# When weight halves are loaded and rounded in the first batch of a spectral mixing and SwiGLU kernel

## The chip, the cores and the metric

The kernel runs on one core of one Trainium2 chip. The metric is the device time of one execution in microseconds (us). Engine names are those of the profile: PE is TensorE (PEld its weight loads), DVE is VectorE, ACT is ScalarE, POOL is GpSimd, SP is SyncE; ACTq and SPq are instructions by which ACT and SP issue DMA transfers.

## What is computed

The reference has two parts, one after the other. `x` has shape (8, 3008, 256), the weights have 256 x 1536 and 1536 x 256 elements.

```python
X = np.fft.rfft(x, axis=1)
y = np.fft.irfft(X * (filt_r + 1j * filt_i)[None], n=3008, axis=1)
t = y.reshape(24064, 256)
g = t @ w_gate
out = (g / (1 + np.exp(-g)) * (t @ w_val)) @ w_out
```

The reference's weights are double precision numbers. The kernel reads them as pairs of 32-bit words and rounds them to single precision itself.

## The kernel before

**The transform.** The length 3008 is 47 x 64. A `Spectral` object stands for one of the 8 batches. Stage 1 (`stage1`; `stage1_first` and `turn` for batch 0) and stage 2 (`stage2a`: product with a table, then with the filter; `stage2b`: product with a second table) write their result to DRAM as `d2`: `stage2b(u)` copies its sum to a buffer `g` on ACT and stores it, 12 stores for a batch, each of eight rows of `d2_rows`, which has 96. `load_t4` reads `d2_rows` back and `stage3` makes the inverse transform over 47 from it, in four steps for each group of tokens: step s has token half i = s // 2 and channel half cb = s % 2. A step with cb = 0 is copied by ACT to the first four parts of the tile `y`; a step with cb = 1 is combined with those by DVE and ACT into the last four parts.

**The feed forward layer.** The products with `w_val`, `w_gate` and `w_out` are made by a fast bilinear scheme: sums and differences of parts of `y` (the tile `y_t`, by `combine_sequence`) are multiplied with sums and differences of weights (`wt_t`, and in batch 0 also `lent`). One pass over a group of tokens `k` and a third `g` of the hidden units is a step of 12 in a batch, and its order is written out by hand in the list `SCHEDULE` of 150 tokens: `P`, `Q`, `A`, `B`, `E` are products (L731: `wk`, `wa`, `we`), `f`, `c`, `m`, `D`, `x`, `s`, `y`, `e`, `l`, `g`, `u`, `h`, `v`, `S` are the work of ACT, DVE and POOL on them, `W` and `o` the projection with `w_out` (L810 and the sums behind it), and `t` runs a piece of the next batch's transform. Batch 0 takes its first nine steps as (0,0), (1,0), (2,0), (0,1), (1,1), (2,1), (0,2), (1,2), (2,2) in (k, g).

**The weights in batch 0.** The weights come in 36 halves of 256 KB: for each of three groups eight halves of hidden weights and four of `w_out`. `load_weights(i)` fetches half i, `round_half(i)` rounds it in pieces, separated by `yield`. Halves 0 to 11 (`N_EARLY`) are loaded early by SyncE; the others are loaded by a DMA instruction in ACT's queue. From half 12 on three of five use places in the tail of `wo_t` (`spot_of`) and the others, with all of the last four halves (`N_LENT` is 32), two buffers `raw`. The last four halves are `w_out`.

`Preparation` lays all of this out in ticks: each half has a start `b`, its pieces run at fixed ticks after `b`, and its load stands some ticks before. The class writes it so:

```python
gap = 4 if i != 2 * len(BLOCKS) and i != len(weights) - 2 else 8
b = base[-1] + gap if i else 0
...
last = base[same[-k]] + 8 if same[k - 1:] else 0
put(max(last, b - 10), lambda i=i: load_weights(i), by)
```

`same[-k]` is the half that used the buffer before. Eight ticks are run by stage 1 of batch 0, 24 by its stage 2 loop, the rest up to tick 46 by `preparation.finish(0)`, and after that 20 ticks in each step, spread evenly over the tokens; tick 100 is not run before step 3, so that step 3 begins at tick 100, step 4 at 120, step 5 at 140 and step 6 at 160.

**The start of batch 0.** SyncE issues, in this order: the input `x`, tables and the first eight halves, `wi_t`, halves 8 to 11, and then the stores of `stage2b` for u up to 9 (the others stand in ACT's queue). Then it loads `d2` back in two parts: rows 0 to 79 and rows 80 to 95 (`load_t4` with `part`). While these come, TensorE runs products that only keep it busy (`warm`, `idle`).

Engines work through their queues in the order in which the code gives them (`pin`). Of SyncE's later work the transfers that matter here are `load_x` (L482), the stores and reloads of `y` (L922, L926), of sums (L929, L932), of rounded weights (L371) and of partial outputs (L695, L794).

Of the kernel before, what the change touches and what calls it, by code (L numbers as in the profile page):

```python
# [56 lines left out]
NK = 4 * NS  # L57
# [6 lines left out]
NT = 3  # L64
NG = 3
# [6 lines left out]
N_TWO = NS // NV  # L72
# [27 lines left out]
BLOCKS = (0, 1, 3, 2)  # L100
# [44 lines left out]
def kernel(  # L145
# [10 lines left out]
    nc = tc.nc  # L156
    wf_host, wi_host, de_host = dft_tables()
    wf_dram = nc.inline_tensor(wf_host, name="wf_tbl")
    wi_dram = nc.inline_tensor(wi_host, name="wi_tbl")
# [17 lines left out]
    wi_t = cpool.tile([NK, NR], FP32)  # L177
# [44 lines left out]
    pin = tc.keep_in_program_order  # L222
# [37 lines left out]
    weights = list(weight_halves())  # L260
    raws = {}
# [12 lines left out]
    N_EARLY = 12  # L274

    def load_weights(i):
        if i in raws or i >= len(weights):
            return
        if i < N_EARLY:
            raws[i] = early_raw(i)  # L280
        elif spot_of(i) is not None:
            raws[i] = bits(4 * 7 * 128 + 512 * spot_of(i))
        else:
            raws[i] = rpool.tile([128, 2, 128, 2], U32, name=f"raw_{i}", tag="raw", bufs=2)
        queue = nc.sync if i < N_EARLY else nc.scalar
        pin(queue.dma_start(out=raws[i], in_=weights[i][0]))

    def round_half(i):


        raw, (use, *at) = raws[i], weights[i][1]
        low, high = raw[:, :, :, 0], raw[:, :, :, 1]
        pw = rpool.tile([128, 2, 128], U32, name=f"pw_{i}", tag="pw", bufs=3)
        if i % 3 == 2 and i < N_LENT:
            w = wo_t.rearrange("p j i f -> p (j i f)")[:, NJ * 7 * 128 - 256:]
            w = w.rearrange("p (b f) -> p b f", b=2)
        else:
            w = rpool.tile([128, 2, 128], FP32, name=f"w_{i}", tag="w", bufs=2)
        man = w.bitcast(U32)
        v = nc.vector  # L300
        flat = "p b f -> p (b f)"
        flat2 = "p b f two -> p (b f) two"
        pin(v.tensor_scalar(out=man, in0=high, scalar1=0xFFFFF, scalar2=None,
                            op0=ALU.bitwise_and))
        yield
        pin(v.tensor_scalar(out=pw, in0=high, scalar1=20, scalar2=0x7FF,
                            op0=ALU.logical_shift_right, op1=ALU.bitwise_and))
        pin(nc.scalar.activation(out=w, in_=man, func=AF.Copy, scale=2.0 ** -20, bias=1.0))
        yield
        pf = pw.bitcast(FP32)  # L310
        pin(nc.scalar.activation(out=pf, in_=pw, func=AF.Relu, bias=off_t))
        pin(nc.scalar.activation(out=pf, in_=pf, func=AF.Relu, bias=top_t, scale=-1.0))
        yield
        pin(nc.scalar.activation(out=pw, in_=pf, func=AF.Copy, scale=-(2.0 ** 23),
                                 bias=255 * 2.0 ** 23))
        yield
        pin(v.scalar_tensor_tensor(out=pw.rearrange(flat), in0=raw.rearrange(flat2)[:, :, 1],
                                   scalar=0x80000000, in1=pw.rearrange(flat),
                                   op0=ALU.bitwise_and, op1=ALU.bitwise_or))
        yield  # L320
        pin(v.scalar_tensor_tensor(out=w.rearrange(flat), in0=raw.rearrange(flat2)[:, :, 0],
                                   scalar=2.0 ** -52, in1=w.rearrange(flat),
                                   op0=ALU.mult, op1=ALU.add))
        yield
        e = nc.gpsimd
        if use == "proj":
            j, l = at
            dst = wo_t[:, j]
            pin(e.tensor_tensor(out=dst[:, ts(l, 2), :], in0=w, in1=pf, op=ALU.mult))
            yield  # L330
            if l:
                b11, b12, b21, b22, t1, t2, t4 = [dst[:, i] for i in range(7)]
                pin(sub(e, t1, b12, b11))
                pin(sub(e, t2, b22, t1))
                pin(sub(e, b12, b22, b12))
                pin(sub(e, t4, b21, t2))
            return
        g, i, z = at
        wt = weights_of(0, 0, g)
        x, y, u = w[:, 0], wt[:, SLOT[f"Q{i}"], z], wt[:, SLOT[f"P{i}"], z]  # L340
        pin(e.tensor_tensor(out=y, in0=w[:, 1], in1=pf[:, 1], op=ALU.mult))
        pin(e.tensor_tensor(out=x if KS[i] else u, in0=x, in1=pf[:, 0], op=ALU.mult))
        yield
        if KS[i] == -1:
            pin(sub(e, u, x, y))
        elif KS[i]:
            pin(add(e, u, x, y))
            if KS[i] == 2:
                pin(add(e, u, u, y))
# [27 lines left out]
    class Preparation:  # L377
# [3 lines left out]
        def __init__(self):  # L381
            self.at, self.held = 0, []

            self.ticks, self.need = {}, {}
            base, ready = [], {}

            def put(t, f, by, pool=False):
                self.ticks.setdefault(t, ([], []))[pool].append(f)
                self.need[by] = max(self.need.get(by, 0), t)

            for i, (_, (use, *at)) in enumerate(weights):
                hid, g = use == "hid", at[0] if use == "hid" else at[0] // JB
                by = ((0, 3, 6) if hid else (1, 4, 7))[g]
                gap = 4 if i != 2 * len(BLOCKS) and i != len(weights) - 2 else 8
                b = base[-1] + gap if i else 0
                base.append(b)
                if hid and g == NG - 1:
                    ready.setdefault(NT, b)
                if i >= N_EARLY:
                    same = [n for n in range(N_EARLY, i) if spot_of(n) == spot_of(i)]  # L400
                    k = 2 if spot_of(i) is None else 1
                    last = base[same[-k]] + 8 if same[k - 1:] else 0
                    put(max(last, b - 10), lambda i=i: load_weights(i), by)
                half = []

                def go(half=half, i=i):
                    if not half:
                        half.append(round_half(i))
                    next(half[0], None)

                for n, t in enumerate((0, 1, 2, 3, 6, 7, 9, 10)):
                    put(b + t, go, by, n > 5)
                if hid and at[1:] == [BLOCKS[-1], 1]:
                    for n, pair in enumerate(PAIRS_USED):
                        c = combine_weights(g, *pair)
                        for t in range(3):
                            put(b + 11 + n + t, lambda c=c: next(c, None), by, t == 2)
            self.barriers = sorted((t, step) for step, t in ready.items())
            self.end = max(self.ticks)
# [50 lines left out]
    class Spectral:  # L470
# [59 lines left out]
        def load_t4(self, k, i, part=None):  # L530
            if part is not None:

                t = f0[0:NK, ts(i, NH), :]
                r = (slice(0, NK - 16), slice(NK - 16, NK))[part]
                self.load(out=t[r], in_=self.d2_rows[r, ts(i, NH), :])
            else:
                t = t4pool.tile([NK, NH, C], FP32, name=f"t4_{self.b}_{k}_{i}", tag="t4")
                self.load(out=t, in_=self.d2_rows[:, ts(2 * k + i, NH), :])
            self.t4[k, i] = t
# [78 lines left out]
        def stage2b(self, u):  # L618

            pt, tb = self.p.pop(u), self.tb.pop(u)  # L620
            ps = self.bank(f"pc_{self.b}_{u}")
            for i in range(NV):
                pin(nc.tensor.matmul(out=ps[:, i, :], lhsT=tb[:, i, 1, :],  # L623
                                     rhs=pt[:, i, :], start=True, stop=True))
            g = self.place("g", u)
            yield
            pin(nc.scalar.copy(out=g, in_=ps))
            queue = nc.scalar if self.b or u > N_TWO - 3 else nc.sync
            pin(queue.dma_start(out=self.twos(self.d2, u), in_=g))

        def stage3(self, k, step):
# [207 lines left out]
    with tc.tile_pool(name="start", bufs=1) as spool0:  # L839
# [12 lines left out]
        n = 0  # L852
# [23 lines left out]
                ("w", 7), ("t", 5)]  # L876
        for what, i in load:
            {"x": spec.load_x, "w": load_weights, "t": spec.load_tables}[what](i)
        pin(nc.sync.dma_start(out=wi_t, in_=wi_dram.ap()))
        for u in range(8):  # L880
            if u in (4, 6):
                idle(zero, [bank("idle") for _ in range(2)], 512)
            spec.stage1_first(u)
            if u > 3:
                preparation.tick(0, 2)
        for i in range(8, N_EARLY):
            load_weights(i)
        for u in range(2):
            spec.turn(u)
        lag = 3  # L890
        for u in range(N_TWO + lag):
            if u < N_TWO:
                spec.turn(u + 2)
                step = spec.stage2a(u)
# [5 lines left out]
                spec.real_part(u + 1)  # L900
            if u >= lag:
                run(spec.stage2b(u - lag))
            if u == N_TWO:
                for i in range(2):
                    spec.load_t4(0, i, 0)
        for i in range(2):
# [2 lines left out]
            spec.load_t4(1, i)  # L909
        preparation.finish(0)  # L910
        warm()
        for step in range(4):
            run(spec.stage3(0, step))
        idle(zero, [bank("idle") for _ in range(3)], 512)
        following = Spectral(1)
# [77 lines left out]
    for b in range(B):  # L993
# [33 lines left out]
        for step in range(NCHUNK * NG + (b == B - 1)):  # L1027
# [17 lines left out]
            for place, token in enumerate(SCHEDULE):  # L1045
# [5 lines left out]
                if op[0] == "t":  # L1051
                    n = int(op[1])
# [60 lines left out]
```

## Time and profile before

| | |
|---|---|
| time, median of 3 | 2984.84 us (2982.82 to 2984.92) |
| span of the profiled run | 2983.5 us |
| PE busy | 2932.4 us (98%) |
| DVE, ACT, POOL busy | 1929.5, 1616.7, 1584.0 us |
| bytes read from and written to HBM | 459.73 MB and 95.05 MB |

A line of a timeline has the start, the length, the engine, the line of the code, the operation, what it writes and reads, the shapes, how many such instructions were merged (x), and in brackets how long the engine stood idle before it and what released it. A line of the windows has the stretch, its length, the busy time and number of instructions of PE, PEld, DVE, ACT and POOL, the TensorE clock that was granted (1.00 is full), the share of the 16 DMA engines and GB/s. In the page the span is cut into 40 slices of 75 us; each digit is a share in tenths.

Step 0 of batch 0 begins at about 88 us; steps 1 to 6 begin at 117.1, 151.65, 187.14, 218.29, 264.18 and 301.66 us.

### The profile page before, as it was taken

To read this page: it belongs to the slowest core of one execution; us is meant where nothing else is said; L and a number is where in the kernel's file an instruction comes from. 1 tells how busy PE (TensorE), PEld (TensorE's weight loads), DVE (VectorE), ACT (ScalarE), POOL (GpSimd) and SP (SyncE) were. 2 spreads that over 40 slices of the span, in tenths; PEclk is the share of its full clock that TensorE was granted. 3 is DMA by queue.
4 is the path that set the end of the run, shared out by engine and by line. 5 is a ranking of instruction groups with operands and counts; after the bars stand their busy time and mean duration, and the time that the engine had idled before them with its cause. 6 is when DMAs were issued, how large, how long until landed. Compare 5 with 4: busy or idle time off the path is not lost.

```text
span 2983.5 us, 57655 instructions
## 1 busy us (share of the span) xinstructions
PE 2932.4 (98%) x20292; PEld 2832.4 (95%) x20292; DVE 1929.5 (65%) x4379; ACT 1616.7 (54%) x4207; POOL 1584.0 (53%) x1764
## 2 busy tenths in 40 slices
PE   7898999999999999999999999999999999999999
PEld 5887999999999999999999999999999999999999
DVE  6786775566655766557665577656676566666665
ACT  5775455555555555555555555555545555555554
POOL 3875564454554555455644464545564545555453
PEclk9998999999999999999999999999999999999999
DMA  8575875565645665556555566556665565644442
GB/s 209 184 259 182 270 248 170 176 211 184 209 154 191 206 200 173 180 183 219 180 178 182 186 216 196 168 179 192 199 204 165 178 201 187 207 151 146 142 135 89
DMA packets 217082, 558.60 MB, mean 187 GB/s; under 512 B 29872, under 2 KB 107552, under 8 KB 216512
## 3 DMA queue, kind: packets, MB, share of 16 engines
q1 hardware_dynamic: 165994, 479.82, 50.8%
q10 hardware_dynamic: 41872, 51.20, 5.1%
q0 software_dynamic: 8928, 23.89, 2.3%
q8 instruction: 163, 2.67, 0.4%
q14 instruction: 125, 1.02, 0.1%
HBM read 459.73 MB, written 95.05 MB: 186 GB/s over the span
## 4 chain that ended last, share of the span: by engine, by line
PE 89%; DMA 0%; DVE 0%; SPq 0%; issue 0%; ACT 0%; POOL 0%; ACTq 0%; DVEq 0%
PE wa L731 23%; PE wA L810 16%; PE wk L731 15%; PE we L731 12%; PE wG L810 8%; PE wF L810 4%; PE pd L639 3%; PE pa L551 3%; PE pc L623 2%; PE pb L591 2%; DMA lent<-de_tbl 0%; DMA y<-y 0%; DVE o L225 0%; POOL D L228 0%; SPq L695 0%
## 5 line engine op out<-in xcount | busy, mean ns | idle before, releaser
L731 PE MATMUL wa<-y_t,wt_t 128*128 128x188 f32 x4464 | 882.0, 324 | 10.3 <-ACT m L766 3.3
L731 PEld LDWEIGHTS wa<-y_t,wt_t 128*128 128x128 f32 x4464 | 731.4, 190 | 36.0 <-issue 16.3
L225 POOL TENSOR_TENSOR h<-h 128x376 f32<-128x376 f32 x190 | 183.0, 985 | 797.6 <-DVE h L778 797.6
L810 PE MATMUL wA<-wo_t,h 128*128 128x128 f32 x4608 | 579.2, 276 | 2.4 <-DVE o L225 2.0
L810 PEld LDWEIGHTS wA<-wo_t,h 128*128 128x128 f32 x4608 | 564.0, 192 | 16.7 <-issue 10.7
L731 PE MATMUL wk<-y,wt_t 128*128 128x188 f32 x2976 | 567.2, 323 | 0.0
L228 POOL TENSOR_TENSOR h<-h 128x376 f32<-128x376 f32 x570 | 554.5, 995 | 0.5
L731 PEld LDWEIGHTS wk<-y,wt_t 128*128 128x128 f32 x2976 | 478.6, 190 | 25.7 <-issue 20.2
L228 DVE TENSOR_TENSOR we<-we,m 128x376 f32<-128x376 f32 x576 | 318.5, 556 | 196.2 <-PE we L731 140.3
L731 PE MATMUL we<-y_t,wt_t 128*128 128x188 f32 x2232 | 431.5, 323 | 0.1
L731 PEld LDWEIGHTS we<-y_t,wt_t 128*128 128x128 f32 x2232 | 369.5, 190 | 0.6 <-DVE we L232 0.4
L228 POOL TENSOR_TENSOR D<-f,f 128x376 f32<-128x376 f32 x288 | 280.3, 987 | 105.4 <-ACT f L746 104.7
L232 DVE SCALAR_TENSOR_TENSOR y<-wk,c 128x376 f32<-128x376 f32 x480 | 244.9, 542 | 134.8 <-ACT we L762 84.8
L766 ACT COPY m<-wa 128x376 f32<-128x376 f32 x576 | 272.0, 472 | 87.7 <-PE wa L731 86.6
L773 ACT ACTIVATE g<-wa 128x188 f32<-128x188 f32 x576 | 188.2, 327 | 191.1 <-PE wa L731 181.7
L810 PE MATMUL wG<-wo_t,h 128*128 128x128 f32 x2304 | 289.9, 276 | 0.6 <-DVE o L225 0.6
L773 ACT ACTIVATE u<-we 128x188 f32<-128x188 f32 x576 | 189.2, 328 | 175.5 <-DVE we L228 156.3
L810 PEld LDWEIGHTS wG<-wo_t,h 128*128 128x128 f32 x2304 | 283.1, 193 | 1.0 <-DVE o L225 0.8
L746 ACT ACTIVATE f<-wk 128x376 f32<-128x376 f32 x288 | 139.4, 484 | 238.9 <-PE wk L731 209.2
L750 ACT COPY c<-wk 128x376 f32<-128x376 f32 x288 | 136.2, 473 | 226.4 <-PE wk L731 226.4
L753 DVE SCALAR_TENSOR_TENSOR x<-wk,f 128x376 f32<-128x376 f32 x192 | 104.3, 543 | 233.6 <-PE wk L731 230.8
L762 ACT COPY we<-y 128x376 f32<-128x376 f32 x480 | 223.7, 486 | 31.8 <-DVE h L778 14.5
(140 smaller groups left out, 3945.1 us busy)
## 6 DMA issues: line engine op xcount, KB each, us to landing
wt_t<-w_all SPq DMA_DIRECT2D x174, 896.0 KB
wt_t<-w_all SPq DMA_DIRECT2D x174, 768.0 KB
t<-d SPq DMA_DIRECT2D x62, 384.0 KB
d<-t ACTq DMA_DIRECT2D x112, 192.0 KB
lent<-de_tbl SPq DMA_DIRECT2D x84, 256.0 KB
lent<-in_filt_r_dram SPq DMA_DIRECT2D x336, 64.0 KB
lent<-d SPq DMA_DIRECT2D x84, 256.0 KB
d<-lent ACTq DMA_DIRECT2D x84, 256.0 KB
```

Of the source, the lines that this page charges most:

```text
L225: return eng.tensor_tensor(out=dst, in0=a, in1=b, op=ALU.add)
L228: return eng.tensor_tensor(out=dst, in0=a, in1=b, op=ALU.subtract)
L232: return nc.vector.scalar_tensor_tensor(out=dst, in0=a, scalar=-1.0, in1=b, op0=ALU.mult, op1=ALU.subtract)
L551: pin(nc.tensor.matmul(out=ps[0:NK], lhsT=wf_t, rhs=self.x.pop(u), start=True, stop=True))
L731: pin(nc.tensor.matmul(out=ps[:, z], lhsT=self.wt[:, SLOT[p], z], rhs=rhs, start=start and z == 0, stop=True, skip_group_check=True))
L746: pin(act.mul(self.small(f"f{i}", f"f{i}", 1), t[f"k{i}"], -1.0))
L750: pin(act.copy(out=self.small(f"c{i}", f"c{i}", 1), in_=t[f"k{i}"]))
L753: pin(v.scalar_tensor_tensor(out=dst, in0=t[f"k{j}"], scalar=-1.0, in1=t[f"f{i}" if j == 3 else f"D{at}"], op0=ALU.mult, op1=ALU.add))
L762: pin(act.copy(out=self.bank(f"e{at}"), in_=t[f"y{at}"]))
L766: pin(act.copy(out=self.small(f"m{at}", "m", 4), in_=t[f"a{at}"]))
L773: pin(act.activation(out=self.small(op, "g", 3, 1)[:, 0], in_=ps[:, 1], func=AF.Silu))
L810: pin(nc.tensor.matmul(out=self.tiles[at][:, t, :], lhsT=self.hs[i][:, HID[p], t0:t0 + 128], rhs=wo_t[:, JB * q + i, WO[p], :], start=star ...
```

## The change

All parts concern batch 0. (1) All halves are loaded by SyncE. (2) The start `b` of a half is put at least 8 ticks behind the tick of its load, which moves the last four halves. (3) The two Relu operations of the rounding are a tick apart, and the Copy that follows is a tick later. (4) `wi_t` and halves 8 to 11 are loaded in the middle of the stage 2 loop, so behind the first stores of `d2`. (5) Stores from u = 8 on go through ACT's queue, and `d2` is read back as rows 0 to 63, one iteration earlier, and rows 64 to 95. (6) The four steps of stage 3 for the first tokens run by channel half: 0, 2, 1, 3.

```diff
-        queue = nc.sync if i < N_EARLY else nc.scalar
-        pin(queue.dma_start(out=raws[i], in_=weights[i][0]))
+        pin(nc.sync.dma_start(out=raws[i], in_=weights[i][0]))
...
         pin(nc.scalar.activation(out=pf, in_=pw, func=AF.Relu, bias=off_t))
+        yield
         pin(nc.scalar.activation(out=pf, in_=pf, func=AF.Relu, bias=top_t, scale=-1.0))
...
-                gap = 4 if i != 2 * len(BLOCKS) and i != len(weights) - 2 else 8
-                b = base[-1] + gap if i else 0
-                base.append(b)
-                if hid and g == NG - 1:
-                    ready.setdefault(NT, b)
+                b = base[-1] + (4 if i != 2 * len(BLOCKS) else 8) if i else 0
                 if i >= N_EARLY:
                     same = [n for n in range(N_EARLY, i) if spot_of(n) == spot_of(i)]
                     k = 2 if spot_of(i) is None else 1
                     last = base[same[-k]] + 8 if same[k - 1:] else 0
+                    b = max(b, last + 8)
                     put(max(last, b - 10), lambda i=i: load_weights(i), by)
+                base.append(b)
+                if hid and g == NG - 1:
+                    ready.setdefault(NT, b)
...
-                for n, t in enumerate((0, 1, 2, 3, 6, 7, 9, 10)):
-                    put(b + t, go, by, n > 5)
+                for n, t in enumerate((0, 1, 2, 3, 4, 6, 7, 9, 10)):
+                    put(b + t, go, by, n > 6)
...
-                r = (slice(0, NK - 16), slice(NK - 16, NK))[part]
+                r = (slice(0, 64), slice(64, NK))[part]
...
-            queue = nc.scalar if self.b or u > N_TWO - 3 else nc.sync
+            queue = nc.scalar if self.b or u >= 8 else nc.sync
...
-        pin(nc.sync.dma_start(out=wi_t, in_=wi_dram.ap()))
...
-        for i in range(8, N_EARLY):
-            load_weights(i)
...
-            if u == N_TWO:
+            if u == 6:
+                pin(nc.sync.dma_start(out=wi_t, in_=wi_dram.ap()))
+                for i in range(8, N_EARLY):
+                    load_weights(i)
+            if u == N_TWO - 1:
                 for i in range(2):
                     spec.load_t4(0, i, 0)
...
-        for step in range(4):
+        for step in (0, 2, 1, 3):
             run(spec.stage3(0, step))
```

## The prediction

> **What bounds the kernel now.** I read the page's engine row first, then its slices, then the windows cut at the steps of the first batch, then every matmul group that had to wait, and last what the engine named there was doing.
>
> The page, engine row and two rows of slices:
>
> ```profile
> PE 2932.4 (98%) x20292; PEld 2832.4 (95%) x20292; DVE 1929.5 (65%) x4379; ACT 1616.7 (54%) x4207; POOL 1584.0 (53%) x1764
> ...
> PE   7898999999999999999999999999999999999999
> ...
> PEclk9998999999999999999999999999999999999999
> ```
>
> TensorE is the bound; it is idle for 2983.5 - 2932.4 = 51 us in all, and the idle and the lower clock lie in the first four slices (300 us). From 300 to 2900 us it is busy 2597.95 of 2600. So only the first batch can give anything. Its steps, each from its first `wk` product to the next step's (columns: stretch, its length, busy of each engine, granted clock, DMA share, GB/s):
>
> ```profile
> 117.10:151.65 34.55, 31.36 (x225) 30.08 (x224) 28.78 (x59) 26.97 (x72) 29.00 (x37) 1.00 0.64 208
> 151.65:187.14 35.49, 32.10 (x225) 30.08 (x223) 32.02 (x69) 25.08 (x68) 31.79 (x42) 1.00 0.68 218
> 187.14:218.29 31.15, 30.70 (x200) 27.84 (x199) 22.90 (x54) 23.47 (x61) 18.12 (x25) 1.00 0.87 301
> 218.29:264.18 45.89, 35.77 (x201) 31.86 (x199) 28.46 (x66) 24.41 (x66) 19.47 (x29) 0.86 0.65 215
> 264.18:301.66 37.48, 32.89 (x195) 30.34 (x195) 25.74 (x56) 18.59 (x49) 25.68 (x35) 0.90 0.46 149
> ```
>
> Steps 3 and 4 have the same products (200 and 201 records), yet step 4 takes 45.89 us against 31.15, at clock 0.86. The waiting matmuls of steps 4 and 5, from the timeline of PE (in brackets: idle before, released by):
>
> ```profile
> 248.11 1.62 PE L731 MATMUL we<-y_t,lent 128*128 128x188 f32 x4 [6.40 <-DVE we L232]
> 258.95 1.62 PE L731 MATMUL we<-y_t,lent 128*128 128x188 f32 x4 [2.95 <-ACT we L762]
> 284.68 0.90 PE L731 MATMUL wa<-y_t,lent 128*128 128x188 f32 x4 [3.52 <-ACT wa L757]
> ```
>
> The DVE instructions in front of the first two, from the timeline of DVE, and the load that the first waits for, from that of ACT:
>
> ```profile
> 246.84 0.29 DVE L303 TENSOR_SCALAR w<-raw 128x256 uint32<-128x256 uint32 x1 [7.51 <-DMA raw<-in_moe_w_out_dram]
> 257.78 0.29 DVE L303 TENSOR_SCALAR w<-raw 128x256 uint32<-128x256 uint32 x1 [6.09 <-DMA raw<-in_moe_w_out_dram]
> ```
> ```profile
> 238.97 0.36 ACTq L286 DMA_DIRECT2D raw<-in_moe_w_out_dram  x1
> ```
>
> VectorE reaches the first operation of rounding a half of `w_out` and stands until that half has landed: 246.84 - 238.97 = 7.9 us after its issue; the second, issued at 251.53, takes 6.25 us. Everything queued behind on VectorE, the `we` sums TensorE needs among it, stands too. These are halves 32 and 33, by the tick arithmetic below.
>
> **What the Trainium skill says.** "TensorE: Matmul & The Clock Gate", Architectural detail: ACT and DVE are strict FIFO, so one early instruction that waits for a load holds all behind it; the 7.51 us above agree. The same page, Part 1 (the HAM clock gate): after an idle window of about 3.4 us the clock is halved until some 3.4 us of work have passed; the trace agrees, with four products at 1.62 us instead of 0.80 after the 6.40 us gap. "DMA: Bandwidth & Descriptors", Issuing engines are not separate DMA queues: which engine issues saves only its issue time. So moving loads to SyncE makes no load faster. The same page, Queues, rings and completion order: one queue's ring is taken in order, so a half on SyncE's queue comes behind the larger transfers issued before it there. The trace has no half of 12 or above on that queue; I bound this below.
>
> **The rounding schedule (steps 4 and 5).** A half starts at tick b; halves from 12 on are loaded at max(last, b - 10), where last = start of the half that used its buffer before, plus 8. With 4 ticks between halves and 8 before half 8, half 30 starts at tick 124 and half 31 at 128. Halves 32 to 35 have only the two `raw` buffers, so half 32 follows half 30: last = 132 = its own start. Load and first use share a tick, likewise for half 33 (136). Halves 34 and 35 have 4 ticks (140 to 144, 144 to 148). After the change b is at least last + 8: starts 140, 144, 156, 160, loads 132, 136, 148, 152. No earlier half moves: reuse there is already 16 ticks or more. A step has 20 ticks and lasts 31.15 us, so 8 ticks are 12.5 us, against landings of 7.9 and 6.25 us. Both waits go.
>
> Step 4 then costs what step 3 does: 45.89 - 31.15 = **14.7 us** (idle 6.40 + 2.95 and small ones, the rest clock).
>
> Step 5 without waits is step 3 less two `pa` pairs at 0.86 us: 29.4, so there are 37.48 - 29.4 = 8.1 us in it. Its 3.52 us gap comes through VectorE from GpSimd (`D` at 282.56), which is busy without a break from 263.15 to 284.4: 21.3 us, of which 3.4 are two `proj` products (L329) and four subtractions of `w_out` that now come later; the twelve combinations of the hidden weights stay in the same ticks. `D` thus comes some 3.4 us sooner, but TensorE, no longer slow at 261 to 265 us, comes 1.7 us sooner too. Instead of 3.52 + 0.78 us idle and 3 us of low clock I leave 1.5 us: **6.6 us**. The work moved reaches ten ticks into step 6, which has no wait now and has DVE at 23.3 of 31 us; I charge **0.5 us** there.
>
> **Loads on SyncE.** 24 DMA issues of 0.35 to 0.42 us leave ACT; SyncE gets them. What matters is what each waits behind there. The longest waits of SyncE before 300 us are `yt` stores for GpSimd (13.1 and 11.9 us), `y_t` reloads for TensorE (7.6), `t` and `x` loads for TensorE (10.8 at most). Placed in program order among SyncE's issue times: half 20 goes after the store of 134.81 (ACT issued it at 137.41), half 25 after 169.11 (171.98), half 26 after 177.66 (179.92), half 31 after 215.24 + 1.94 (215.46, first used at 232). None is issued over 2 us later than now, and all have 15 us to first use. Half 32 goes before the store of 236.88 and has 1.5 MB ahead in the ring (two `o` of 384 KB, `y` of 752 KB): at 215 to 300 GB/s 5 to 7 us, then its own 1.2; 8.2 us are inside 12.5. The bounds are 0 and about 3 us of wait for both halves; I take 0. What stands behind a load on SyncE are `x`, `y` and `o` loads, which have a step's time.
>
> On ACT the removed issues, and the second Relu one tick away from the first (0.51 us each), shorten its queue before the `m` and `wa` copies, which end waits of 0.22, 0.69, 0.81, 0.57, 1.04 and 0.45 us in steps 0 to 3: 3.8 us together. The rest of that region's waits (GpSimd 1.96, `h` 1.39, issue 0.61 and 1.19) is untouched. I take a quarter: **1.0 us**; bounds 0 and 3.
>
> **The start.** In the stage 2 loop TensorE loses 3.89 us before 61.50 because ACT stands 3.31 us at 60.38 (copy of `g`, waiting for an earlier `d` store). That store was queued on SyncE behind `wi_t` and the four `w_out` loads and issued only at 55.59, though SyncE had its tables out by 49.88 and the first `g` was ready at 42.3. After the change stores 0 to 3 go first. VectorE paces this loop and loses 1.92 us at 65.29 against its usual 0.70: gain 1.2. The Copy (L314), now one tick later, leaves the queue ahead of the filter copies (L616) at two of these places, 0.4 us each: 0.8. The last rows: now 64 of 96 are fetched before the end, and stores 8 to 11 go by ACT. The fetch of the rest doubles to 128 KB each, but the 640 KB that shared the engines with the last store (issued 75.20, its rows read from 80.24) are gone. It stays hidden either way: the 28 warming products fill TensorE until 82.53, so I cost it at nothing. Stage 3 by channel half lets ACT copy both base halves back to back; the `y_t` sums at 88.50 wait for the last of these chains, and start some 0.4 us sooner. Sum **2.4 us**.
>
> Total: 14.7 + 6.6 - 0.5 + 1.0 + 2.4 = 24.2; 2984.84 - 24.2 = **2960.6 us**.
>
> **Rivals.**
> A. GpSimd stays the limit of step 5: its combinations all fall in ticks 141 to 146, beside the `S` sums, and the 3.52 gap with its slow clock stays. For: 20 us of unbroken GpSimd work; against: 3.4 us less of it. Gain 24.2 - 6.6 = 17.6: 2967.
> B. The smoother ACT queue shortens more of the waits in steps 0 to 3, and step 5 keeps none: 24.2 + 2 + 1.5 + 1 = 28.7: 2956.
> C. Transfers take the place: from step 6 on DMA is at 0.83 and a `y` reload ends a wait at 389.32 us; if that chain kept its time, the gain would come back as idle there: 2984. Against: the chain starts at SyncE instructions that TensorE releases (370.9), so it moves along.
> D. Slower: SyncE's waits make the halves late. Each late half holds VectorE; the 20 halves before 32 would have to wait 1.5 us each, with the stalls of 32 and 33 replaced in kind, for 2984.84 - 24.2 + 30 = 2991. Against: the issue times above.
>
> **How the numbers follow.** Forecast 0.64, A 0.20, B 0.10, C 0.03, D 0.03. The forecast's own spread is 2957 to 2965 (3 us of steps 0 to 3, 1.5 of step 5, some of step 6). The range 2954 to 2969 takes in A and B. Faster by over 0.2% (under 2978.9) are the forecast, A and B: 0.94; same C: 0.03; slower D: 0.03.
>
> **What would show it.** Right: no DVE L303 waiting for DMA; step 4 near 31 us at clock 1.00; step 5 at 30 to 32; the `g` copy of ACT with no 3.31 us wait; everything after 300 us as now, shifted. Wrong: L303 waiting for `raw` on DMA at other halves; a `D` wait of 3 us in step 5; new idle of TensorE in step 6; or the shift shrinking after 332 us.

## The result and the profile after

The changed kernel takes 2965.49 us (median of 4 runs, 2962.57 to 2969.85) against 2984.88 us of the kernel before beside it: a ratio of 0.9935, 95% interval 0.9918 to 0.9953, so 19.4 us less. The forecast was 2960.6, the range 2954 to 2969.

The page after, engine row and the slices of PE and its clock:

```profile
PE 2928.8 (99%) x20292; PEld 2829.5 (95%) x20292; DVE 1929.7 (65%) x4379; ACT 1610.3 (54%) x4207; POOL 1584.8 (53%) x1764
...
PE   8899999999999999999999999999999999999999
...
PEclk8999999999999999999999999999999999999999
```

The work is the same to the instruction (x20292); the low clock in slice 4 (225 to 300 us) is gone, and one has come in slice 1, of which more below. The windows of steps 1 to 6, columns as before:

```profile
120.91:154.76 33.85, 31.87 (x224) 30.11 (x223) 28.59 (x62) 25.51 (x73) 29.31 (x37) 1.00 0.63 209
154.76:190.58 35.82, 32.59 (x224) 30.03 (x223) 31.02 (x66) 24.49 (x67) 32.08 (x43) 1.00 0.67 218
190.58:220.82 30.24, 30.24 (x200) 27.70 (x199) 24.12 (x58) 23.54 (x65) 18.57 (x26) 1.00 0.86 294
220.82:251.06 30.24, 30.24 (x200) 27.70 (x199) 25.41 (x57) 20.20 (x54) 18.48 (x28) 1.00 0.85 292
251.06:282.71 31.65, 29.54 (x197) 26.92 (x195) 25.97 (x57) 19.33 (x53) 23.48 (x30) 1.00 0.67 224
282.71:314.70 31.99, 30.48 (x210) 29.71 (x209) 26.78 (x56) 15.84 (x42) 17.79 (x21) 1.00 0.81 261
```

Step 4 is 30.24 us, as long as step 3, with TensorE busy throughout. Step 5 is 31.65. What TensorE still waits for, from the timeline of PE (steps 5, 6 and 8):

```profile
262.81 1.51 PE L731 MATMUL wa<-y_t,lent 128*128 128x188 f32 x8 [0.74 <-PE wk L731]
264.66 1.58 PE L810 MATMUL wA<-wo_t,h 128*128 128x128 f32 x12 [0.34 <-DVE o L225]
269.18 0.90 PE L731 MATMUL wa<-y_t,lent 128*128 128x188 f32 x4 [0.81 <-ACT wa L757]
270.31 1.60 PE L810 MATMUL wA<-wo_t,h 128*128 128x128 f32 x12 [0.22 <-DVE o L225]
...
296.49 1.58 PE L810 MATMUL wA<-wo_t,h 128*128 128x128 f32 x12 [1.51 <-DVE o L225]
354.56 1.10 PE L591 MATMUL pb<-lent 128*128 128x256 f32 x4 [1.44 <-DMA lent<-d]
373.92 0.90 PE L731 MATMUL wa<-y_t,wt_t 128*128 128x188 f32 x4 [2.69 <-ACT wa L757]
```

The 6.40, 2.95 and 3.52 us of before are gone. In their place stand 2.1 us in step 5, 1.5 in step 6 and 4.1 in step 8.

**How the runs below are compared.** Runs of one kernel lie up to 10 us apart (2981.68 to 2991.43 in 31 runs of before), so beside the totals the profile of each run is cut at the same products: the first transposing product (`wpt`), the first `wk`, and from step 1 on the first `wF` of each step, which follows the step's first `wk` by 0.64 us. The columns are us from the start to `wpt`; from `wpt` to the end of step 0; steps 1 to 3 together; steps 4, 5, 6 and 8. Step 7 is 30.25 in all. The last column is the median's distance from the median of before in the same comparison. All columns but the last come from one profile of each kernel. The text ahead of each result is what was expected of that run; the names of the theories and rivals come from there.

| kernel | to wpt | wpt to end of 0 | 1 to 3 | 4 | 5 | 6 | 8 | total |
|---|---|---|---|---|---|---|---|---|
| before | 26.25 | 90.86 | 101.18 | 46.33 | 37.04 | 30.82 | 32.71 | |
| changed | 31.69 | 89.21 | 99.92 | 30.25 | 31.64 | 31.99 | 35.09 | -19.4 |
| changed again (c0) | 27.17 | 90.91 | 99.16 | 30.24 | 31.64 | 32.00 | 35.50 | -19.7 |
| e1, part 2 alone | 26.36 | 91.59 | 101.25 | 31.40 | 31.78 | 31.98 | 33.22 | -19.1 |
| e2, all but part 2 | 26.57 | 89.19 | 99.93 | 37.53 | 38.89 | 30.81 | 33.26 | -9.9 |
| e3, part 1 alone | 27.25 | 91.63 | 99.93 | 37.83 | 38.42 | 30.82 | 33.45 | -7.1 |
| e5, parts 4 and 5 alone | 26.18 | 91.18 | 101.22 | 43.32 | 37.98 | 30.82 | 36.65 | -1.0 |
| e6, part 3 alone | 26.62 | 89.90 | 99.97 | 42.70 | 39.47 | 30.81 | 34.61 | -2.0 |
| e7, part 6 alone | 27.06 | 91.08 | 100.84 | 45.16 | 37.05 | 30.80 | 34.43 | -1.2 |
| e4, changed, Copy sooner | 26.06 | 89.62 | 100.96 | 30.30 | 31.62 | 31.97 | 34.57 | -20.8 |
| e8, changed, y sooner | 26.20 | 89.25 | 99.93 | 30.24 | 31.63 | 32.00 | 32.12 | -23.7 |
| e9, changed, combinations apart | 26.44 | 89.21 | 99.90 | 30.25 | 29.19 | 31.99 | 37.10 | -24.3 |
| e10, e8 and e9 together | 26.30 | 89.22 | 100.03 | 30.24 | 29.21 | 32.51 | 32.76 | -27.2 |
| e11, e10 and e4 together | 26.99 | 87.94 | 101.66 | 30.36 | 29.18 | 31.98 | 32.65 | -25.9 |

### The profile page after: what moved, and what is told of

The parts are those of the page before. It is cut to its first block, busy times and chain, and to the rows that moved or that the text cites. A ratio compares the mean times of both kernels' runs of the same rounds, so it can differ in the third digit from the quotient of the medians.

```text
span 2968.1 us, 57673 instructions
## 1 busy us (share of the span) xinstructions
PE 2928.8 (99%) x20292; PEld 2829.5 (95%) x20292; DVE 1929.7 (65%) x4379; ACT 1610.3 (54%) x4207; POOL 1584.8 (53%) x1764
## 4 chain that ended last, share of the span: by engine, by line
PE 91%; DMA 1%; DVE 1%; POOL 1%; SPq 0%; issue 0%; ACT 0%; ACTq 0%
PE wa L731 24%; PE wA L810 17%; PE wk L731 16%; PE we L731 12%; PE wG L810 8%; PE wF L810 4%; PE pd L639 3%; PE pa L551 3%; PE pc L623 2%; PE pb L591 2%; DMA y<-y 0%; DMA lent<-de_tbl 0%; DMA d<-lent 0%; DMA lent<-in_filt_r_dram 0%; POOL wt_t L225 0%
## 5 line engine op out<-in xcount | busy, mean ns | idle before, releaser
L762 ACT COPY we<-y 128x376 f32<-128x376 f32 x480 | 223.9, 486 | 32.7 <-DVE h L778 14.1
```

The costliest lines, as they stand in the source:

```text
L762: pin(act.copy(out=self.bank(f"e{at}"), in_=t[f"y{at}"]))
```

## The experiments

**Which part brings the gain: e1, e2, e3.** e1 is the kernel before with part 2 alone. Of its edit, the line that moves the starts:

```diff
+                    b = max(b, last + 8)
```

> The kernel before with part 2 of the change alone (a half starts at least 8 ticks behind its load; loads stay on ACT). Theory W (the two waits of VectorE for halves 32 and 33 are nearly all of the gain): steps 4 and 5 take 30 to 31.5 and 31 to 32.5 us, total 20 to 22 us below before, so as fast as the whole change or faster. Rival Q (loads on SyncE are needed for it, since ACT issues them too late): step 4 or 5 keeps a wait of VectorE on a load, gain under 15 us.

It gained 19.1 us (ratio 0.9941, 0.9924 to 0.9957), a little under the 20 to 22 expected. The windows of its steps 3, 4 and 5, and VectorE's first operation on half 32, with no wait in front of it:

```profile
187.99:219.19 31.20, 30.73 (x200) 27.85 (x199) 22.93 (x54) 23.63 (x62) 18.16 (x25) 1.00 0.87 305
219.19:250.60 31.41, 31.12 (x200) 27.79 (x199) 26.51 (x60) 21.53 (x58) 18.80 (x28) 1.00 0.78 264
250.60:282.38 31.78, 30.17 (x196) 27.04 (x195) 25.76 (x57) 19.86 (x53) 23.30 (x30) 1.00 0.70 221
```
```profile
251.44 1.06 DVE L303 TENSOR_SCALAR w<-raw 128x256 uint32<-128x256 uint32 x1
```

Step 4 costs what step 3 does, at full clock, as the prediction has it. Part 2 alone gives, within what the medians can tell, what the whole change gives, and for part 2 the rival Q falls: loads issued by ACT (this one at 239.39) are in time.

e2 is the changed kernel with part 2 undone.

> The changed kernel with part 2 undone (starts as before). Theory W: steps 4 and 5 are at 43 to 47 and 35 to 38 us again and nearly the whole gain is lost: within 4 us of before. Rival Q: loads issued by SyncE, ahead of ACT's queue, come early enough, and at least a third of the gain stays (7 us or more).

Here Theory W failed, and the rival's figure, at least 7 us, came true: 9.9 us of the gain stayed (0.9972, 0.9961 to 0.9983). Steps 4 and 5 took 37.53 and 38.89, 6.9 us less together than before. The loads still come too late (VectorE waits 5.88 and 4.48 us for them), but less so. e3 shows which part does it: the kernel before with part 1 alone.

```diff
-        queue = nc.sync if i < N_EARLY else nc.scalar
-        pin(queue.dma_start(out=raws[i], in_=weights[i][0]))
+        pin(nc.sync.dma_start(out=raws[i], in_=weights[i][0]))
```

> The kernel before with part 1 alone (all loads on SyncE). Theory W: within 3 us of before, steps 0 to 3 shorter by 0 to 2 us from a shorter ACT queue; waits for halves 32 and 33 stay. Rival: SyncE's own waits hold loads back and the steps get longer by 3 us or more.

Theory W failed here too. The kernel gained 7.1 us (0.9975, 0.9967 to 0.9983), as much as steps 4 and 5 got shorter: 46.33 + 37.04 = 83.37 before, 37.83 + 38.42 = 76.25 here (81.30 to 82.21 in e5, e6 and e7, which also leave these loads to ACT). The waits are there, but shorter. From e3's timelines of DVE and of SyncE's queue (L302 and L285 are the L303 and L286 of before, L370 its L371, the store of rounded weights):

```profile
243.51 0.29 DVE L302 TENSOR_SCALAR w<-raw 128x256 uint32<-128x256 uint32 x1 [4.71 <-DMA raw<-in_moe_w_out_dram]
...
252.75 0.29 DVE L302 TENSOR_SCALAR w<-raw 128x256 uint32<-128x256 uint32 x1 [4.43 <-DMA raw<-in_moe_w_out_dram]
```
```profile
237.91 0.33 SPq L285 DMA_DIRECT2D raw<-in_moe_w_out_dram  x1
238.34 0.41 SPq L370 DMA_DIRECT2D w_all<-lent  x1
...
247.34 0.35 SPq L285 DMA_DIRECT2D raw<-in_moe_w_out_dram  x1
247.79 0.45 SPq L370 DMA_DIRECT2D w_all<-lent  x1
```

The halves take 243.51 - 237.91 = 5.6 and 252.75 - 247.34 = 5.4 us from issue to first use, where ACT's took 7.9 and 6.25. The other profiles agree: the two times add up to 11.0 us in e3 and 11.8 in e2, and to 14.1 to 14.3 in the four kernels that leave these loads to ACT and their starts as before (before, e5, e6, e7). The two waits fall from 13.6 to 9.1 us, 3.1 us of it by the shorter times and the rest because SyncE issued the loads a little sooner before VectorE came to them; TensorE's gaps fall from 6.40 and 2.95 to 3.60 and 0.32, and behind the second its clock stays up (0.91 us for four products, not 1.62). A likely reason is in the same lines: on SyncE the load goes in front of a 768 KB store, while before that store was issued at 236.88 and ACT's load at 238.97, behind it. That this order, and not something else in the queues, makes the difference was not tried by itself.

Parts 1 and 2 thus work on the same waits; with part 2 in place little is left to gain there (step 4: 31.40 in e1, 30.25 in the changed kernel, parts 1 and 3 to 6 together).

**The start: e4 to e7.** In the changed kernel VectorE stands 5 us at the end of the stage 2 loop for the Copy (L314) of half 7, which part 3 put a tick later. The timelines of DVE and ACT of the changed kernel:

```profile
80.34 0.42 DVE L317 SCALAR_TENSOR_TENSOR pw<-wt_t,pw 128x256 uint32<-128x256 uint32 x1 [5.05 <-ACT pw L314]
```
```profile
78.87 0.58 ACT L627 COPY x<-wpc 128x512 f32<-128x512 f32 x1 [2.54 <-PE wpc L623]
...
79.89 0.42 ACT L314 ACTIVATE pw<-pw 128x256 uint32<-128x256 f32 x1 [0.44 <-ACT x L627]
```

The Copy has crossed the end of the loop and stands behind the last copy of `g`, which waits for TensorE. e4 puts it back on the tick of the second Relu.

```diff
-                for n, t in enumerate((0, 1, 2, 3, 4, 6, 7, 9, 10)):
+                for n, t in enumerate((0, 1, 2, 3, 3, 6, 7, 9, 10)):
```

> The changed kernel with the rounding's Copy (L314) on the tick of the second Relu, as before, and only the two Relu apart. Theory L (the later Copy of the last half of the loop stands in ACT's queue behind the last copies of g, and VectorE waits 5.05 us for it, which costs about 2.4 us before step 0): that wait is gone, and from the first transposing product to step 0 it takes 59 to 60 us where the changed kernel takes 61.9; total 1.5 to 3 us below the changed kernel. Rival: VectorE has to wait for GpSimd or the last rows then, and nothing is gained (61 to 62 us).

The wait went, and step 0 began 59.89 us after `wpt` instead of 61.86, as Theory L has it; but the changed kernel's other profile, c0, which has the wait of 5.05 us, began it after 60.57. Step 0 then took 29.73 us instead of 27.35, steps 1 to 3 took 100.96 instead of 99.92, and the total (0.9935, 0.9920 to 0.9950) is that of the changed kernel. The edit is not confined to the start: it puts the Copy of every half back, so the loss in steps 1 to 3 can be its own. What the head start alone is worth stays open.

e5 has parts 4 and 5 alone.

> The kernel before with parts 4 and 5 alone (late loads of wi_t and halves 8 to 11, stores from u = 8 on by ACT, rows in two parts 64 and 32). Theory S: ACT's wait of 3.3 us for an earlier store of d2 is gone; from the first transposing product to the end of step 0 it takes 89 to 90 us (before, and in e1 and e3, which leave the start as it was, 90.9 to 91.6); total 0 to 2 us below before. Rival: the wait is gone but the way to the end of step 0 stays at 90.9 or more, since something else paces it.

The rival's figures came true. ACT's wait of 3.31 us for the store is gone and step 0 begins after 60.02 us (before: 62.51), but step 0 takes 31.16 us instead of 28.35 and the total is unchanged (0.9998, 0.9990 to 1.0007). That the wait is gone does not show that parts 4 and 5 removed it: e1 and e3, which have the old order, have no such wait either, e6 has 1.20 us of it and e7 1.81. SyncE came to the stores behind `wi_t` and the four loads at 50.97 us in e1 and 53.01 in e3, and only at 55.59 in the profile of before. Its first longer wait in step 0, from e5's timeline of PE:

```profile
96.93 2.51 PE L731 MATMUL wa<-y_t,wt_t 128*128 128x188 f32 x8 [3.46 <-DVE wa L753]
```

In the kernel before that wait is 1.75 us; VectorE in turn waits there for GpSimd's `D` (1.89 us), behind GpSimd's sums of `y_t`. So the likely pace of this stretch is GpSimd's; no run changed that alone.

e6 has part 3 alone.

> The kernel before with part 3 alone (the second Relu and the Copy a tick later each). Theory L: VectorE waits about 5 us for the Copy of half 7 at the end of the stage 2 loop, step 0 begins 2 us later after the first transposing product (64 us or more), and steps 1 to 3 are together 1 to 2 us shorter (before: 101.2 us). Rival: the start and the steps are as before within 0.7 us.

VectorE's wait for the Copy came (5.0 us), yet step 0 began after 61.78 us, not 64: that half of Theory L fell. (This time varies by itself: with the start as it was it is 62.51 us in before, 61.34 in e3, 61.83 in e7 and 65.33 in e1.) Steps 1 to 3 took 99.97 us instead of 101.18, 1.2 less, as expected. The total (0.9993, 0.9985 to 1.0002) can't be told from before.

e7 has part 6 alone.

> The kernel before with part 6 alone (stage 3 by channel half). By the prediction's term the way to the end of step 0 is 0.4 us shorter than the 90.9 to 91.6 us of the kernels that leave the start as it was; the rival says 0. The total can't tell these apart; the stretches of the trace may.

91.08 us to the end of step 0, total 0.9995 (0.9986 to 1.0004): no gain that can be told.

**What is left in step 5 and step 8: e8, e9, e10.** They ran beside the changed kernel:

> The changed kernel once more, beside the next three. It should stand 18 to 21 us below before; step 8 (products from 315 to 350 us on) at 33.5 to 35 us with waits of TensorE for a transfer and for the copy of y sums.

It gave 0.9936 (0.9924 to 0.9949) and 35.50 us for step 8, a little over what was expected. e8 moves the reload of `y` in step 8:

```diff
-        chore(step, "A02", lambda s: reload_y(order_of(0)[s + 1][0], s), step)
+        chore(step, "A02" if step < NT * NG - 1 else "Q2",
+              lambda s: reload_y(order_of(0)[s + 1][0], s), step)
```

> The changed kernel with one line moved: in step 8 the reload of y for the next step is issued at token Q2, ahead of the weight reloads, instead of at A02. Theory Y (the wait of ACT for the y reload, 7.8 us after its issue, is what makes step 8 long): the wait of TensorE for ACT's wa copy (1.7 to 2.7 us) is gone, step 8 is 1.5 to 2.5 us shorter, the total 1 to 2.5 us lower than the changed kernel. Rival B (bandwidth: the 16 DMA engines are the limit there, so the order is indifferent): the wait moves to another transfer and step 8 stays at 33.5 to 35.

Theory Y held, with more than it foresaw: step 8 takes 32.12 us, 3.4 less than in c0, and the total fell to 2962.54 us (0.9923, 0.9909 to 0.9936; runs 2961.53 to 2962.93, all below the 2963.74 to 2969.62 of c0). What ACT waits for in front of the first sum of the reloaded `y`, in the changed kernel and in e8:

```profile
372.35 0.92 ACT L682 ACTIVATE y_t<-y 128x376 f32<-128x376 f32 x2 [4.23 <-DMA y<-y]
```
```profile
363.82 0.92 ACT L682 ACTIVATE y_t<-y 128x376 f32<-128x376 f32 x2 [2.27 <-PE we L731]
```

The releaser changes from the transfer to TensorE, so ACT now waits for the engine it serves, and TensorE's wait of 2.69 us is gone from the step. The reload is issued at 348.52 us here, 15.3 us before this use; in the changed kernel it was 364.46, 7.9 us before.

e9 spreads GpSimd's combinations of the last hidden weights.

```diff
-                            put(b + 11 + n + t, lambda c=c: next(c, None), by, t == 2)
+                            put(b + 11 + (3 if g == NG - 1 else 1) * n + t,
+                                lambda c=c: next(c, None), by, t == 2)
```

> The changed kernel with the twelve GpSimd combinations of the third group of hidden weights spread over ticks 141 to 156 instead of 141 to 146. Theory G (GpSimd's backlog from them is what is left of step 5's waits, 2.1 us in all): these waits fall below 0.7 us and step 5 goes from 31.6 to 30 to 30.5 us; step 6, whose products need these weights, unchanged. Rival: the waits stay, since VectorE and not GpSimd sets them, or return at the start of step 6.

Theory G held: step 5 takes 29.19 us and its four waits of TensorE are gone; 2961.96 us (0.9921, 0.9908 to 0.9935), although step 8 had one of its long passages (37.10). GpSimd's `D` in step 5, in the changed kernel (whose step starts at 251.06) and in e9 (245.80):

```profile
261.14 0.98 POOL L228 TENSOR_TENSOR D<-f,f 128x376 f32<-128x376 f32 x1
267.06 1.92 POOL L228 TENSOR_TENSOR D<-f,f 128x376 f32<-128x376 f32 x2
```
```profile
252.27 1.00 POOL L228 TENSOR_TENSOR D<-f,f 128x376 f32<-128x376 f32 x1
255.34 1.03 POOL L228 TENSOR_TENSOR D<-f,f 128x376 f32<-128x376 f32 x1
```

It comes 10.1 and 16.0 us after the step's start there and 6.5 and 9.5 here, and VectorE's waits for it, 0.84 and 2.93 us, are gone. Step 6 stays at 31.99 us.

e10 has both.

> The changed kernel with both edits, e8 and e9. If both theories hold the effects add: 2 to 4 us below the changed kernel; if neither does, the same.

2959.06 us (0.9912, 0.9899 to 0.9926; 2958.43 to 2960.28): 7.4 us below the changed kernel beside it, more than the 2 to 4 expected. This is the best version. e11 adds e4's edit.

> The changed kernel with the edits of e8, e9 and e4 together. If the earlier Copy (e4) gains nothing because step 0 waits for other things, it is within 1 us of e10's 27 us below before; if those 2 us were only hidden by noise in e4, it is about 2 us below that.

2960.67 us (0.9916, 0.9901 to 0.9931): no further gain. Step 0 ends 1.3 us sooner than in e10 (87.94 for 89.22), and steps 1 to 3 take 1.6 us more (101.66 for 100.03), as they did in e4.

## Why the prediction was right, and which terms were off

The main mechanism is right and shown: the three terms that belong to part 2 add up to 20.8 us, and part 2 alone gave 19.1. The other two terms, 3.4 us for the start and ACT's queue, are hardly to be seen in the medians: the whole change is 19.4 and 19.7 us below before. In the profiles, from `wpt` to the end of step 8, the changed kernel is 3.1 us ahead of e1, and c0 1.8.

**Halves 32 and 33.** Right, and shown: e1 has part 2 alone and all of the gain. Step 4 came out at 30.25 us for the 31.15 foreseen, because step 3 itself fell to 30.24. The term of 14.7 us measures 46.33 - 30.25 = 16.1 against that one profile of before; in the runs that leave these waits to ACT's loads step 4 is anywhere from 42.70 to 46.33.

**Step 5.** Foreseen 6.6 us, measured 37.04 - 31.64 = 5.4. `D` was to come 3.4 us sooner; counted from the step's start its later place went from 282.56 - 264.18 = 18.4 us to 16.0, so 2.4 sooner. The mechanism (GpSimd's combinations hold `D`) was named in rival A and e9 shows it; what the prediction left over, 1.5 us, was 2.1 us of waits and is 31.64 - 29.19 = 2.45 us of time. The length without waits, 29.4, measures 29.19.

**Step 6.** Charged 0.5 us; measured 31.97 to 32.00 against 30.82, so 1.2, in every run with part 2, e1 included (e10: 32.51). TensorE's wait of 1.51 us there is the new idle of step 6 that the prediction gave as a sign of being wrong.

**Loads on SyncE.** The step that failed is "moving loads to SyncE makes no load faster". That nothing comes late was right. But e3 gained 7.1 us from this part alone. The Trainium skill ("DMA: Bandwidth & Descriptors", Issuing engines are not separate DMA queues) says that several issuers save only issue time; the measured 5.6 and 5.4 us against 7.9 and 6.25 show that here the load's way got shorter too, by its place among larger transfers as far as the lines suggest. The prediction's own estimate for half 32 on this queue was up to 8.2 us. The forecast was not hurt only because part 2 takes the same waits away.

**ACT's shorter queue.** 1.0 us foreseen for steps 0 to 3. Steps 1 to 3 gained 1.3 us, and e3 and e6 show that either part 1 or part 3 gives about this alone (99.93, 99.97). It goes on in step 4, which is 1.15 us shorter than in e1.

**The start.** The term of 2.4 us is the one that is not borne out as argued. The store wait that it set out from comes and goes with the old order too, and parts 4 and 5 alone, and part 6 alone, bring nothing that can be told at the end of step 0: in e5 the time won before step 0 is given back in it. The later Copy, counted as a gain of 0.8 us, left VectorE a wait of 5.05. Yet something came: to the end of step 0 five profiles with parts 1 and 3 to 6 (changed, e2, e8, e9, e10; their other edits lie later) take 89.19 to 89.25 us and a sixth (c0) 90.91, while the five kernels without part 3 take 90.86 to 91.63. Of the parts tried alone only part 3 has some of this (e6: 89.90), and by what way was not tried.

**After 300 us.** Foreseen "as now, shifted". Step 8 took 2.4 us more in the changed profile, so the shift shrank after 332 us, another of the prediction's signs of being wrong, as a weak form of rival C would have it. But e5, with steps 4 and 5 hardly moved, has 36.65, e6 34.61, e7 34.43: the step varies with the landing of its transfers (`y` in most profiles, `d` in e6, `yt` in c0), and the profile of before had the shortest passage of the kernels without e8's edit (32.71). So this is no proven cost of the change.

The sum from the profiles is 1.65 + 1.26 + 16.08 + 5.40 - 1.17 - 2.38 = 20.8 us, less the 5.4 us that the changed profile lost before `wpt`, where TensorE's code is unchanged; the medians say 19.4. Against the 24.2 foreseen most of what is missing is in step 5, step 6, the start and step 8.

## What to carry to other kernels

Find the first instruction of each strict queue that waits for a load, and compare the distance between issue and use with the landing time in the trace: here a distance of zero cost 15 us on an engine that was 65% busy, and eight ticks of 1.5 us cured it. Two parts of a change that work on the same wait each look large alone (19.1 and 7.1 us) and do not add. Before paying for an earlier start, look whether the next stage waits for another engine; and before naming a wait as the cause, look whether it stands in a second profile of the same code.

## What the runs showed that was not expected

TensorE's code of the first 26 us is the same in all kernels, yet took 26.06 to 27.25 us in thirteen profiles and 31.69 in the fourteenth, that of the changed kernel. From its timeline of PE and its windows:

```profile
8.86 10.92 PE L564 MATMUL wpa<-wf_t,wo_t 94*128 94x96 f32 x60 [0.94 <-DMA wo_t<-in_x_dram]
```
```profile
4.42:11.24 6.82, 5.88 (x33) 4.07 (x32) 0.79 (x1) 0.82 (x1) 0.00 (x0) 1.00 1.05 230
11.24:21.48 10.24, 10.24 (x44) 9.21 (x44) 2.44 (x4) 2.41 (x3) 0.00 (x0) 0.50 1.03 216
21.48:31.69 10.21, 9.79 (x71) 8.19 (x70) 3.52 (x8) 4.98 (x10) 0.00 (x0) 1.00 1.08 210
```

One piece of the input landed late and TensorE stood 0.94 us. From 11.24 us on its clock was halved for 10.24 us, although it was busy all that time, and then full again. Half a clock for 10.24 us is 5.1 us of work lost, most of the 5.4 us by which this profile is behind that of before.

So what the prediction took for the clock, about 3.4 us of idle before it is halved and some 3.4 us of work until it is back, fits the gap of 6.40 us but not this one. The length of a gap does not decide it alone either: behind the 2.95 us gap of before four products took 1.62 us and the clock was back after about 6 us, while behind the 2.69 us gap in step 8 of the changed kernel four products took 0.90. What decides it was not tried.
